# Window attention with sinks, then a highway layer: five placements changed in one hand-ordered instruction stream

## The chip, the cores and the metric

The kernel runs on one core of one Trainium2 chip. The metric is the device time of one execution in microseconds (us), given as a median over several runs. The core has a matrix engine (TensorE, in the profile PE for products and PEld for its weight loads), a vector engine (VectorE, DVE), an activation engine (ScalarE, ACT), a general engine (GpSimd, POOL) and a queue engine (SyncE, SP). Each of them takes its own instructions in order; DMA transfers are issued by POOL, SP and ACT.

## The reference

Four batches of eight heads, 768 positions, 64 values a head. A query at position i may look at the keys 0 to 3 (the sinks) and at the keys i-127 to i. What comes out is laid side by side for the eight heads, 3072 rows of 512, and goes through a highway layer.

```python
scores = scale * np.matmul(q, k.transpose(0, 1, 3, 2))
keep = is_sink | in_window
scores = np.where(keep, scores, -1000000000.0)
a = np.exp(scores - np.max(scores, axis=-1, keepdims=True))
a = a / (np.sum(a, axis=-1, keepdims=True) + 1e-09)
x = np.matmul(a, v)                       # then (tokens, 512)
H = np.maximum(x @ w_h, 0.0)
T = 1.0 / (1.0 + np.exp(-(x @ w_t + b_t)))
out = T * H + (1.0 - T) * x
```

## The kernel before, in words

The rows are cut into 24 tiles of 128 (n = 0 to 23, six for each batch b, c = n mod 6 within it). A tile goes through these steps, each a small function that the diff and the prediction name:

- `load_part`, `load_whole`, `load_v`, `load_v_third`: DMAs that POOL issues (L123, L130, L168, L161); they turn fp32 into fp16 on the way. `thirds[3]`, `thirds[4]` and `thirds[5]` are the three loads of v of batch 1.
- `transpose_qk` (L148) and `transpose_tiles` (L155): DVE turns q and k in 32x32 blocks.
- `scores` (L303, PE, into the one score buffer `ps_s`), `expo` (L334, ACT, from `ps_s` into `E`), `mask` (L342, DVE, `E` times a 0/1 mask, in place).
- `values` (L371 and L374, PE: the tile before and the tile itself times v, with a column of ones that gives the sum) and `values_of_sinks` (L357, PE: the sinks' part, for tiles with c of 2 or more), both into `ps_v`; `norm` (L383, L384, DVE) divides by the sum and gives `X`.
- `x_transpose` (L411, PE), `x_copy` (L416, ACT), `bias` and `gate` (L421, L425, PE, with the weights `wt`, into `ps_z`), `tanh` (L449, ACT), `hidden` (L465, PE, with `wh`, into `ps_h`), `diff` (L469, DVE; for some tiles L477 on ACT and L480 on DVE), the gate's value (`gate_on_act`, L455, on ACT or `gate_value`, L460, on POOL), `gated` (L483, DVE), `add` (L487, POOL), `store` (L491, SP).

For the sinks there are three helpers. `sink_keys(b)` (L264) lays out the keys of the sinks for `sink_scores` (L316), which scores four tiles of a batch at once at the loop step whose n2 is 3 past the batch's first tile. `sink_values(b)` (L280) multiplies the sinks' rows of v, which lie in `vs_rows`, by a mask and writes the 128x520 tile `vs[b]`; `values_of_sinks` reads it from the batch's third tile on. `keep_warm(n)` (L212) issues n products of zeros on PE.

The order of every engine is the order of the text: a last pass ties each instruction to the one before it on its engine. So the program is written out by hand for tiles 0 to 5 (the head), runs as a loop from s = 5 to 21 in which tile n2 = s+2 is scored, n1 = s+1 gets its values, n0 = s its gate and hidden products and n9 = s-1, n8 = s-2 are finished, and is written out again for the last two tiles. In the loop, POOL does in each step `add(n8)`, `gate_value(n9)`, and then what the tables `keys` and `loads` hold for n2.

In the head POOL issues a list of loads (`fill`) in two pieces. The second piece contains `sink_values(2)` ahead of the four loads of k's first half of batch 1 and `sink_values(3)` ahead of the fourth of these. The DMAs that POOL issues count on eight completion counters in turn, so each of them waits for the DMA that was issued eight before it.

Around the change, DVE's order in the head is `norm(1)`, `mask(2)`, `transpose_qk(0, 2, 1, 0, 8)` (the third segment of k of batch 0, which holds tiles 4 and 5), `mask(3)`, `norm(2)`, and PE's is `scores(3)`, `x_transpose(1)`, three idle products, `scores(4)`, `values(2)`, `gate(0)`. At the end, the last tile is gated in two halves of 256 columns; the first one's sum goes to POOL and SP, the second one's stays on DVE (L761, L763) and is stored by ACT's queue.

Of the kernel before, what the change touches and what calls it, by code (L numbers as in the profile page):

```python
# [30 lines left out]
def kernel(  # L31
# [14 lines left out]
    pe, act, dve, pool, sp = nc.tensor, nc.scalar, nc.vector, nc.gpsimd, nc.sync  # L46
# [9 lines left out]
    NC = S // P  # L56
    N = B * NC
    KC = DM // P
    G = 4
# [47 lines left out]
    def v_of(n):  # L107
        b, t = divmod(n, NC)
        return vt[b][t % TH3][:, :, t // TH3, :]
# [9 lines left out]
    def load_part(b, i, g, which, into=None, engine=pool):  # L119

        t0, nt = segments[b][which][i]
        into = nat[b][which][i] if into is None else into
        engine.dma_start(  # L123
            out=into[32 * g:32 * g + 32].rearrange("p hg m d -> p hg (m d)"),
            in_=(q, k)[which][b, :, t0:t0 + nt, :].rearrange(
                "(g hg) (r m) d -> g r hg (m d)", g=G, m=nt // 32)[g])
# [12 lines left out]
    def part_loads(b, i, which):  # L139

        return [lambda g=g: load_part(b, i, g, which) for g in range(G)]

    def transpose_qk(b, i, which, lo, hi):

        t0, nt = segments[b][which][i]
        dst = tr[b].bitcast(FP32).rearrange("p w hg t e -> p w hg (t e)")[
            :, which, :, t0:t0 + nt].rearrange("p hg (r m) -> p hg m r", m=nt // 32)
        dve.transpose(out=dst[:, :, lo:hi, :],  # L148
                      in_=nat[b][which][i].bitcast(FP32)[:, :, lo:hi, :])
# [15 lines left out]
    def load_v(n):  # L165

        b, t = divmod(n, NC)
        pool.dma_start(out=v_of(n)[:, :, 0:D],  # L168
                       in_=v[b, :, t * P:(t + 1) * P, :].transpose([1, 0, 2]))
# [40 lines left out]
    def keep_warm(n):  # L210
        for i in range(n):
            pe.matmul(ps_h, lhsT=zeros[:, 0:P], rhs=zeros[:, 0:DM], start=True, stop=True)  # L212
# [20 lines left out]
    for n, tile_v in enumerate([tile_v for of_batch in vt for tile_v in of_batch]):  # L233
        if n < 2:
            dve.memset(tile_v[:, :, :, D:D + 1], 1.0)
        else:
# [5 lines left out]
                       fill=0.0, base=0, pattern=[[1, P]], channel_multiplier=-1)  # L242
    pool.affine_select(out=mask_std[:, P:], in_=mask_std[:, P:], compare_op=ALU.is_ge,
                       fill=0.0, base=-1, pattern=[[-1, P]], channel_multiplier=1)
# [17 lines left out]
    def sink_keys(b, engine=pool):  # L262
        for hg in range(HG):
            engine.tensor_tensor(  # L264
                out=sk[:, b, hg, :, 0:H * NSINK].rearrange("p e (h s) -> p e h s", s=NSINK),
                in0=tr[b][:, 1, hg, 0:NSINK, :].rearrange("p s e -> p e s").unsqueeze(2)
                .to_broadcast([P, 2, H, NSINK]),
                in1=skmask[:, hg].unsqueeze(1).unsqueeze(3)
                .to_broadcast([P, 2, H, NSINK]), op=ALU.mult)
# [9 lines left out]
    def sink_values(b, engine=dve):  # L279
        engine.tensor_tensor(  # L280
            out=vs[b], in0=vs_rows[:, b].unsqueeze(1).to_broadcast([P, H, D + 1]),
            in1=vmask.unsqueeze(2).to_broadcast([P, H, D + 1]), op=ALU.mult)
# [54 lines left out]
    def mask(n):  # L337
        c = n % NC
        nq = 2 if c + 1 < NC else 1
        m = mask_0 if c == 0 else mask_std  # L340
        e3 = E[n].rearrange("p g hg x -> p (g hg) x")[:, :, 0:nq * P]
        return dve.tensor_tensor(  # L342
            out=e3, in0=e3, in1=m[:, 0:nq * P].unsqueeze(1).to_broadcast([P, H, nq * P]),
            op=ALU.mult)


    def av_of(n):
        if n < N - 1:
            return ps_v[:, :, 0:FREE]
        return ps_s[:, 2:4].rearrange("p b hg x -> p b (hg x)")[:, :, 0:FREE]  # L350
# [28 lines left out]
    def norm(n):  # L379
        rec = work.tile([P, 2, HB], FP32, tag="rec", name="rec")  # L380
        X[n] = work.tile([P, 2, HB, D], FP16, tag="X", name="X", bufs=10)
        av = av_of(n).rearrange("p i (j e) -> p i j e", e=D + 1)
        dve.reciprocal(out=rec, in_=av[:, :, :, D])  # L383
        dve.tensor_tensor(out=X[n], in0=av[:, :, :, 0:D],  # L384
                          in1=rec.unsqueeze(3).to_broadcast([P, 2, HB, D]), op=ALU.mult)
# [5 lines left out]
    HALVES = [slice(0, DM // 2), slice(DM // 2, DM)]  # L391

    def z_of(n, cols):
        return ps_z[:, cols] if n < N - 1 or cols == HALVES[1] else ps_v[:, 0, cols]
# [23 lines left out]
    def bias(n, cols=ALL, group=None):  # L418
        lhsT, rhs = (ones, brow) if group is None else (
            ones_g[32 * group:32 * group + 1], brow[32 * group:32 * group + 1])  # L420
        pe.matmul(z_of(n, cols), lhsT=lhsT, rhs=rhs[:, cols], start=True, stop=False)  # L421
# [12 lines left out]
    def outputs(n):  # L434
        TH[n] = work.tile([P, DM], FP16, tag="TH", name="TH", bufs=6)
        DD[n] = work.tile([P, DM], FP16, tag="DD", name="DD", bufs=8)
        if O[n] is None:
            O[n] = work.tile([P, DM], FP32, tag="O", name="O", bufs=10)
# [43 lines left out]
    def gated(n, cols=ALL):  # L482
        return dve.tensor_tensor(out=DD[n][:, cols], in0=DD[n][:, cols], in1=TH[n][:, cols],  # L483
                                 op=ALU.mult)

    def add(n, cols=ALL):
        return pool.tensor_tensor(out=O[n][:, cols], in0=DD[n][:, cols],  # L487
                                  in1=flat(X[n])[:, cols], op=ALU.add)

    def store(n, cols=ALL, after=None):  # L490
        behind(sp.dma_start(out=out[n * P:(n + 1) * P, cols], in_=O[n][:, cols]), after)  # L491

    def finish(n, cols=ALL):
        add(n, cols)
        store(n, cols)
# [21 lines left out]
    def v_thirds(b):  # L517
# [4 lines left out]
        ((6, 1), (7, 3), (8, 3), (9, 2), (10, 1), (11, 2), (12, 2), (13, 2), (14, 2), (15, 2),  # L522
         (16, 1), (17, 1)))

    keys = {8: 1, 12: 2, 18: 3}


    stored = {12: 1, 13: 3, 14: 4, 15: 6, 16: 7, 17: 9, 18: 10, 19: 12, 20: 14, 21: 16, 22: 18,
# [3 lines left out]
    thirds = [None] * TH3 + v_thirds(1)  # L532
    fill = part_loads(0, 1, 0) + part_loads(0, 1, 1)
# [2 lines left out]
        lambda: pool.dma_start(out=wt, in_=moe_w_t.rearrange("(kc p) of -> p kc of", p=P)),  # L536
        lambda: load_v(3), lambda: load_v(4),
        lambda: pool.dma_start(out=wh, in_=moe_w_h.rearrange("(kc p) of -> p kc of", p=P))]
    fill += part_loads(1, 0, 0)
    for work_item in fill:  # L540
        work_item()

    fill = [lambda: sink_values(2, engine=pool)] + part_loads(1, 0, 1)
    fill.insert(4, lambda: sink_values(3, engine=pool))
    fill += [lambda: load_v(5), thirds[3]] + part_loads(1, 1, 0) + [thirds[4]]

    act.copy(out=mask_0, in_=mask_std)
    act.copy(out=mask_0[0:NSINK, :], in_=ones_v.rearrange("p h i o -> p (h i o)")[
# [20 lines left out]
    repeat_sink_values()  # L569
    norm(0)  # L570
    copy_sink_values()
    for work_item in fill:
        work_item()
    sink_expo(0)
    x_transpose(0)
    x_copy(0)
# [6 lines left out]
    outputs(0)  # L583
    norm(1)
    act.copy(out=brow, in_=b32)
    mask(2)
    scores(3)
    expo(3)
    x_transpose(1)
    x_copy(1)  # L590
    transpose_qk(0, 2, 1, 0, 8)
    keep_warm(3)
    scores(4)
    mask(3)
    bias(0, group=3)
# [17 lines left out]
    gate(1)  # L613
    tanh(1, gate_too=False)
    mask(5)
    sink_values(1)
    x_transpose(3)
    x_copy(3)
    gate_on_act(0)
# [39 lines left out]
    thirds[5]()  # L659
    diff(2)  # L660
    gated(2)
    norm(5)
    add(2)
    hidden(3)
# [6 lines left out]
    for s in range(5, N - 2):  # L671


        n2, n1, n0, n9, n8 = s + 2, s + 1, s, s - 1, s - 2
        x_transpose(n0)
        x_copy(n0)

        hidden(n9, parts=range(2, KC))
        if n2 % NC == 3:
            sinks(n2 // NC)  # L680
        if not at_once(n9):
            gate_on_act(n9)
        take_hidden(n9)

        scores(n2)
        bias(n0, group=(n1 % NC + 1) % G)
        values_of_sinks(n1)
        expo(n2)

        if n1 not in ADDED:  # L690
            mask(n1)
        gated(n8)
        if n9 in TAKEN:
            diff_of_taken(n9)
        else:
            diff(n9)
        outputs(n0)
        values(n1)
        gate(n0, parts=range(0, 2))
        norm(n1)  # L700

        if n2 in keys and n2 < NC * 2:
            sink_keys(keys[n2])
        last = add(n8)
        while done < stored.get(n2, 0):
            store(done, after=last)
            done += 1
        gate_value(n9)
        if n2 in keys and n2 >= NC * 2:
            sink_keys(keys[n2])  # L710
        for load in loads[n2]:
            load()
        for piece in pieces[n2]:
            transpose_qk(*piece)
        for part in tiles[n2]:
            transpose_tiles(*part)
        if n2 == N - 1:
            mask(n2)
        gate(n0, parts=range(2, KC))
        tanh(n0, gate_too=at_once(n0))  # L720
        hidden(n0, parts=range(0, 2))

    n1, n0, n9, n8 = N - 1, N - 2, N - 3, N - 4
# [2 lines left out]
    x_copy(n0)  # L726
    hidden(n9, parts=range(2, KC))
    gate_on_act(n9)
    outputs(n1)
    bias(n0, group=(n1 % NC + 1) % G)  # L730
    values_of_sinks(n1)
    bias(n1, HALVES[0], group=(n1 % NC + 3) % G)
    values(n1)
    gated(n8)
    finish(n8)
# [11 lines left out]
    diff(n0)  # L747
    gated(n0)
    finish(n0)
    bias(n1, HALVES[1])  # L750
    for i, cols in enumerate(HALVES):
        gate(n1, cols)
        tanh(n1, cols, gate_too=(i == 0))
        hidden(n1, cols)
        diff(n1, cols)
        if i == 0:
            gated(n1, cols)
            finish(n1, cols)

    cols = HALVES[1]  # L760
    dve.scalar_tensor_tensor(out=DD[n1][:, cols], in0=TH[n1][:, cols], scalar=1.0,  # L761
# [39 lines left out]
```

## Time and profile before

| what | value |
|---|---|
| median of 3 runs | 109.62 us (108.58 to 110.47) |
| profiled execution, its own time | 109.37 us |
| its span | 107.6 us |
| mean clock granted to TensorE | 0.982 |
| busy: PE, DVE, ACT, POOL | 95.7, 93.8, 82.6, 86.0 us |
| `sink_values` on POOL | 2 instructions, 3.1 us |
| `sink_values` on DVE | 2 instructions, 1.4 us |
| `mask`, 128x2048 with the standard mask | 16 instructions, mean 1261 ns |
| idle products of 128x512 | 33, 9.5 us |

The span is what the profiler recorded between the first and the last instruction; the profiled execution took 1.77 us more than that. In a row of the timeline the first number is the start in us from the span's beginning and the second the duration; "x4" is the number of instructions merged into the row, and what stands in brackets is the time the engine sat idle before it and who released it. A busy PE need not be a fast one: its clock has a row of its own on the page.

### The profile page before, as it was taken

The numbers are of one execution on the slowest core, as the hardware profiler recorded it, in microseconds if no ns is written. First come the engines' busy times: TensorE is split into PE (matmuls) and PEld (weight loads), VectorE is DVE, ScalarE is ACT, GpSimd is POOL, SyncE is SP. The second block draws the span as 40 slices with busy tenths as digits, with TensorE's granted clock in tenths as the row PEclk, the third lists the DMA queues.
The fourth block names the chain that finished last, engine by engine and source line by source line (L and its number), as shares of the span: only waits on it lengthen the run. The fifth ranks groups of instructions, "written<-read, shape, count | busy, mean of one in ns | idle before, by whom it ended". The sixth has DMA issues, their size and how long they took to land.

```text
span 107.6 us, 3031 instructions
## 1 busy us (share of the span) xinstructions
PE 95.7 (89%) x1195; PEld 50.7 (47%) x1195; DVE 93.8 (87%) x183; ACT 82.6 (77%) x113; POOL 86.0 (80%) x117
## 2 busy tenths in 40 slices
PE   5996768499998998999999999999999999999900
PEld 2343443344543554556555455565544564554600
DVE  5898899974899779999998999999989999898670
ACT  0943799675765799999979997998799988965900
POOL 6989999637999999998899999998946543664640
PEclk9999999958999999999999999999999999999999
DMA  2999999998899999999999999999999555235441
GB/s 78 271 212 171 138 119 177 176 200 142 81 123 181 186 112 107 157 156 170 112 97 76 211 249 186 217 263 169 235 207 158 201 195 190 100 106 195 173 155 62
DMA packets 45077, 17.53 MB, mean 163 GB/s; under 512 B 38532, under 2 KB 41348, under 8 KB 45064
## 3 DMA queue, kind: packets, MB, share of 16 engines
q0 software_dynamic: 40656, 9.97, 98.0%
q1 hardware_dynamic: 3944, 6.73, 17.7%
q10 hardware_dynamic: 464, 0.66, 2.2%
q8 instruction: 9, 0.15, 0.6%
q14 instruction: 4, 0.03, 0.1%
HBM read 21.01 MB, written 6.29 MB: 254 GB/s over the span
## 4 chain that ended last, share of the span: by engine, by line
PE 55%; DVE 24%; DMA 9%; ACT 3%; issue 3%; POOL 2%; DVEq 0%; POOLq 0%
PE ps_z L425 13%; PE ps_h L465 13%; DVE E L342 7%; PE ps_s L303 7%; PE ps_v L374 6%; PE ps_v L371 6%; DMA v<-in_v_dram 4%; DMA nat<-in_q_dram 4%; DVE X L384 4%; PE ps_v L411 4%; DVE tr L148 3%; DVE DD L483 3%; DVE tr L155 2%; PE ps_z L421 2%; PE ps_v L357 2%
## 5 line engine op out<-in xcount | busy, mean ns | idle before, releaser
L334 ACT ACTIVATE E<-ps_s 128x2048 f16<-128x2048 f32 (+1 forms) x24 | 41.6, 1735 | 5.8 <-PE ps_s L303 5.7
L487 POOL TENSOR_TENSOR O<-DD,X 128x512 f32<-128x512 f16 (+1 forms) x19 | 22.3, 1176 | 13.1 <-DVE DD L483 12.6
L465 PE MATMUL ps_h<-wh,XT 128*128 128x512 f16 (+1 forms) x96 | 27.3, 375 | 0.0
L425 PE MATMUL ps_z<-wt,XT 128*128 128x512 f16 (+1 forms) x96 | 24.8, 382 | 0.0
L342 DVE TENSOR_TENSOR E<-E,mask_std 128x2048 f16<-128x2048 f16 (+1 forms) x20 | 23.1, 1156 | 0.5 <-ACT E L334 0.3
L449 ACT ACTIVATE TH<-ps_z 128x512 f16<-128x512 f32 (+1 forms) x24 | 14.1, 587 | 7.5 <-PE ps_z L425 7.4
L303 PE MATMUL ps_s<-tr 32*128 32x256 f16 (+1 forms) x384 | 14.5, 267 | 3.3 <-DVE tr L148 2.9
L384 DVE TENSOR_TENSOR X<-ps_v,rec 128x512 f16<-128x512 f32 x23 | 15.9, 692 | 0.8
L374 PE MATMUL ps_v<-v,E 128*128 128x65 f16 x184 | 13.7, 195 | 1.0 <-DVE E L342 0.5
L416 ACT COPY XT<-ps_v 128x512 f16<-128x512 f16 x23 | 13.4, 583 | 1.3 <-PE ps_v L411 0.8
L303 PEld LDWEIGHTS <-tr 32*128 32x128 f16 x384 | 7.9, 94 | 12.5 <-issue 6.4
L371 PE MATMUL ps_v<-v,E 128*128 128x65 f16 x152 | 13.3, 196 | 0.4 <-ACT XT L416 0.3
L374 PEld LDWEIGHTS <-E 128*128 128x128 f16 x192 | 11.8, 98 | 3.6 <-DVE E L342 2.5
L371 PEld LDWEIGHTS <-E 128*128 128x128 f16 x160 | 10.8, 98 | 5.1 <-issue 5.1
L148 DVE STREAM_TRANSPOSE tr<-nat 128x512 f32<-128x512 f32 (+1 forms) x14 | 12.7, 947 | 0.5 <-DMA nat<-in_q_dram 0.3
L465 PEld LDWEIGHTS <-XT 128*128 128x128 f16 x100 | 8.9, 98 | 6.1 <-issue 0.2
L123 POOL DMA_DIRECT2D nat<-in_k_dram x16 | 8.9, 566 | 3.5 <-DMA v<-in_v_dram 1.8
L469 DVE SCALAR_TENSOR_TENSOR DD<-ps_h,X 128x512 f16<-128x512 f32 (+1 forms) x16 | 10.6, 665 | 1.0 <-PE ps_h L465 0.8
L425 PEld LDWEIGHTS <-XT 128*128 128x128 f16 x100 | 8.4, 98 | 6.6 <-ACT XT L416 0.3
L161 POOL DMA_DIRECT2D v<-in_v_dram x9 | 10.7, 1190 | 0.0
L483 DVE TENSOR_TENSOR DD<-DD,TH 128x512 f16<-128x512 f16 (+1 forms) x24 | 10.4, 435 | 0.3
L212 PE MATMUL ps_h<-zeros 128*128 128x512 f16 x33 | 9.5, 442 | 1.3 <-DVE ones_v L217 1.3
(89 smaller groups left out, 141.8 us busy)
## 6 DMA issues: line engine op xcount, KB each, us to landing
out_dram<-O SPq DMA_DIRECT2D x18, 256.0 KB
v<-in_v_dram POOLq DMA_DIRECT2D x9, 256.0 KB, 6.4
nat<-in_q_dram POOLq DMA_DIRECT2D x8, 192.0 KB, 5.3
nat<-in_k_dram POOLq DMA_DIRECT2D x8, 192.0 KB, 5.4
out_dram<-first SPq DMA_DIRECT2D x4, 256.0 KB
v<-in_v_dram POOLq DMA_DIRECT2D x6, 128.0 KB, 5.0
nat<-in_q_dram POOLq DMA_DIRECT2D x8, 96.0 KB, 7.5
nat<-in_k_dram POOLq DMA_DIRECT2D x8, 96.0 KB, 4.2
```

The source lines that it names most:

```text
L148: dve.transpose(out=dst[:, :, lo:hi, :], in_=nat[b][which][i].bitcast(FP32)[:, :, lo:hi, :])
L303: pe.matmul(ps_s[:, g, hg, 0:nq * P], lhsT=tr[b][rows, 1, hg, c * P:(c + 1) * P, e], rhs=tr[b][rows, 0, hg, c * P:(c + nq) * P, e], start= ...
L334: act.activation(out=E[n][:, :, :, 0:nq * P], in_=ps_s[:, :, :, 0:nq * P], func=AF.Exp, scale=SCALE)
L342: return dve.tensor_tensor(out=e3, in0=e3, in1=m[:, 0:nq * P].unsqueeze(1).to_broadcast([P, H, nq * P]), op=ALU.mult)
L371: pe.matmul(slot, lhsT=E[n - 1][:, g, hg, P:2 * P], rhs=v_of(n - 1)[:, h, :], start=first, stop=False, skip_group_check=True)
L374: pe.matmul(slot, lhsT=E[n][:, g, hg, 0:P], rhs=v_of(n)[:, h, :], start=first, stop=True, skip_group_check=True)
L384: dve.tensor_tensor(out=X[n], in0=av[:, :, :, 0:D], in1=rec.unsqueeze(3).to_broadcast([P, 2, HB, D]), op=ALU.mult)
L425: pe.matmul(z_of(n, cols), lhsT=XT[n][:, kc * P:(kc + 1) * P], rhs=wt[:, kc, cols], start=False, stop=(kc == KC - 1))
L449: act.activation(out=TH[n][:, cols], in_=z_of(n, cols), func=AF.Tanh, scale=0.5)
L465: pe.matmul(h_of(n, cols), lhsT=XT[n][:, kc * P:(kc + 1) * P], rhs=wh[:, kc, cols], start=(kc == 0), stop=(kc == KC - 1))
L483: return dve.tensor_tensor(out=DD[n][:, cols], in0=DD[n][:, cols], in1=TH[n][:, cols], op=ALU.mult)
L487: return pool.tensor_tensor(out=O[n][:, cols], in0=DD[n][:, cols], in1=flat(X[n])[:, cols], op=ALU.add)
```

## The change

Six things move or are added, and what is computed stays the same:

1. `sink_values(2)` and `sink_values(3)` leave POOL's list of loads in the head. They are issued by POOL in the loop, at n2 = 12 and 18, ahead of that step's loads.
2. `sink_keys(2)` and `sink_keys(3)`, which stood at n2 = 12 and 18, go to n2 = 13 and 19.
3. `sink_values(1)` on DVE moves from behind `mask(5)` to behind `gated(2)`, ahead of `norm(5)`.
4. `transpose_qk(0, 2, 1, 0, 8)` on DVE goes ahead of `mask(2)`.
5. The idle products ahead of `scores(4)` are seven instead of three.
6. At the end, the first half's `bias` of the last tile goes from ahead of `values` to behind the last full `hidden`, and both halves use the plain bias rows; `gated` and `finish` of the first half come behind the second half's `diff`.

```diff
-    keys = {8: 1, 12: 2, 18: 3}
+    keys = {8: 1, 13: 2, 19: 3}
+    rows = {12: 2, 18: 3}
...
-    fill += part_loads(1, 0, 0)
+    fill += part_loads(1, 0, 0) + part_loads(1, 0, 1) + [lambda: load_v(5), thirds[3]]
+    fill += part_loads(1, 1, 0) + [thirds[4]]
...
-    fill = [lambda: sink_values(2, engine=pool)] + part_loads(1, 0, 1)
-    fill.insert(4, lambda: sink_values(3, engine=pool))
-    fill += [lambda: load_v(5), thirds[3]] + part_loads(1, 1, 0) + [thirds[4]]
...
     norm(1)
     act.copy(out=brow, in_=b32)
+    transpose_qk(0, 2, 1, 0, 8)
     mask(2)
     scores(3)
     expo(3)
     x_transpose(1)
     x_copy(1)
-    transpose_qk(0, 2, 1, 0, 8)
-    keep_warm(3)
+    keep_warm(7)
     scores(4)
...
     mask(5)
-    sink_values(1)
...
     gated(2)
+    sink_values(1)
     norm(5)
...
         if n2 in keys and n2 >= NC * 2:
             sink_keys(keys[n2])
+        if n2 in rows:
+            sink_values(rows[n2], engine=pool)
...
-    outputs(n1)
     bias(n0, group=(n1 % NC + 1) % G)
     values_of_sinks(n1)
-    bias(n1, HALVES[0], group=(n1 % NC + 3) % G)
     values(n1)
...
-    bias(n1, HALVES[1])
+    outputs(n1)
+    for cols in HALVES:
+        bias(n1, cols)
     for i, cols in enumerate(HALVES):
         gate(n1, cols)
         tanh(n1, cols, gate_too=(i == 0))
         hidden(n1, cols)
         diff(n1, cols)
-        if i == 0:
-            gated(n1, cols)
-            finish(n1, cols)
+    gated(n1, HALVES[0])
+    finish(n1, HALVES[0])
```

More of the change, by code (lines that the diff above doesn't have):

```diff
@@ L571 @@
     copy_sink_values()
-    for work_item in fill:
-        work_item()
     sink_expo(0)
```

## The prediction

> **What bounds the kernel now.** I read the shares of the chain that ended last first, then the granted clock in 40 slices (2.7 us each).
>
> ```profile
> PEclk9999999958999999999999999999999999999999
> ...
> PE 55%; DVE 24%; DMA 9%; ACT 3%; issue 3%; POOL 2%; DVEq 0%; POOLq 0%
> ```
>
> PE carries most of the chain, DVE a quarter, POOL 2%, so work on POOL costs nothing by itself; it can cost where it gets in the way of DVE or is late for somebody. The clock is full but for one dip, at 21.8 to 25.2 us by finer windows (0.50 granted). So I took the timeline of that stretch.
>
> ```profile
> 17.23 1.99 DVE L342 TENSOR_TENSOR E<-E,mask_std 128x2048 f16<-128x2048 f16 x1
> ...
> 18.06 2.07 POOL L280 TENSOR_TENSOR vs<-vs_rows,vmask 128x520 f16<-128x520 f16 x1
> 19.14 1.09 DVE L148 STREAM_TRANSPOSE tr<-nat 128x512 f32<-128x512 f32 x1
> ...
> 20.29 0.63 PE L303 MATMUL ps_s<-tr 32*128 32x256 f16 x16 [1.64 <-DVE tr L148]
> ...
> 21.10 0.59 POOL L123 DMA_DIRECT2D nat<-in_k_dram  x1 [0.97 <-DMA wt<-in_moe_w_t_dram]
> ...
> 24.61 1.07 POOL L280 TENSOR_TENSOR vs<-vs_rows,vmask 128x520 f16<-128x520 f16 x1
> ```
>
> Two things are to be seen. `mask(2)` took 1.99 us where masks of its size mostly take 1.18 to 1.29, and `sink_values(2)` took 2.07 where the next one took 1.07: they overlap, and both lost. And `scores(4)` waited 1.64 us for the transposition behind that mask; the clock halved 1.5 us after that wait.
>
> For the loop I followed the chain in order of time, and beside it POOL's timeline.
>
> ```profile
> 59.12 1.24 DVE E L342
> ...
> 62.49 1.23 DVE E L342
> 63.77 0.20 PE ps_v L374
> ```
>
> ```profile
> 38.78 2.28 POOL L487 TENSOR_TENSOR first<-DD,X 128x512 f32<-128x512 f16 x2
> ...
> 58.73 0.54 POOL L264 TENSOR_TENSOR sk<-tr,skmask 128x64 f16<-128x64 f16 x2
> ...
> 62.02 0.61 POOL L460 TENSOR_SCALAR TH<-TH 128x512 f16<-128x512 f16 x1
> 62.59 0.76 POOL L130 DMA_DIRECT2D nat<-in_q_dram  x1
> ```
>
> From 57.5 to 63.8, and again from 78.3 to 84.4, the chain is DVE's alone, so whatever lengthens a mask there moves the end. POOL has no idle time from 26.3 to 50 and hardly any from 53.8 to 71. The steps of the loop last 3.4 us.
>
> Last, DVE's timeline at the end.
>
> ```profile
> 102.11 0.94 DVE L483 TENSOR_TENSOR DD<-DD,TH 128x256 f16<-128x256 f16 x1
> 102.97 0.41 DVE L469 SCALAR_TENSOR_TENSOR DD<-ps_h,X 128x256 f16<-128x256 f32 x1
> 103.49 0.59 DVE L761 SCALAR_TENSOR_TENSOR DD<-TH,DD 128x256 f16<-128x256 f16 x1
> ```
>
> A product of 256 columns took 0.94 where 512 columns take 0.41: a POOL sum ran from 101.75 to 102.90, and the product ended 0.15 after it. So a DVE product of two SBUF tiles that starts while POOL computes ends about its own length after POOL.
>
> **The parts.**
>
> *Head, POOL's list.* Taking both products out frees 2.07 + 1.07 us of POOL, but not earlier loads: the load behind the first waits for `wt` (21.10), the one behind the second for an older load too (26.33, after 0.65 of idle). Those waits fill the room, so every later load leaves when it did. Value 0; bounds 0 and -0.65 (the last wait, were it to shrink).
>
> *Head, transposition ahead of `mask(2)`.* Its data (issued up to 11.8, 3.5 to 4.3 to land) is there at 15.4. It would run 17.23 to 18.2, `mask(2)` 18.2 to 19.4 (1.2 without POOL beside it). Then `scores(4)` waits for the score buffer instead, which `expo(3)` (17.73 + 1.88) frees at 19.61: start 19.66, not 20.29, **-0.63**. The seven idle products run from 17.84 at 0.216 each to 19.35, under that same wait: 0. At half clock they would end at 20.85 and cost 1.2; the clock was 1.00 there. PE's idle stretch falls from 1.64 to 0.3, so I take the dip to be gone: `gate(0)` 0.63 shorter, the values, copies and x-transposes behind it some 0.2 each. `gate(0)` needs `wt`, landed about 21.0; `norm(3)`, now at 25.77, would come 1.5 earlier. What is late next is `wh`: issued 15.17, 10.9 to land, so `hidden(0)`, now at 26.99, can't start before 26.1. Head gain at that point: **-0.9**.
>
> The Trainium skill (TensorE: Matmul & The Clock Gate, Part 1) says that the clock halves after an idle window of about 3.4 us. Here it halved after 1.64 us of waiting, though for 3.4 us, so the trace differs on what it takes; taken literally, the idle products would matter in neither kernel.
>
> *What POOL gives back.* POOL's stretch from 26.3 to 50 doesn't move. The mask at 41.52 would start at 40.6, while the second of the sums at 38.78 runs until 41.06, and wait 0.43. Kept of the head: **-0.45** (0 to -0.9). The loads of batch 1 hold: the last of k lands at 39.3 and is turned at 39.7.
>
> *`sink_values(1)` on DVE.* 0.69 leaves a place where DVE waits for PE anyway and goes to 35.0, in front of a 0.57 wait of `norm(5)`: 0, bounds -0.1 and +0.15.
>
> *Loop, `sink_values(2)`.* It takes the place of the 0.54 at 58.73, lasts 1.07, ends at 59.80. The mask at 59.04 on the chain waits for it: 0.76 instead of the 0.14 that it lost to the two short ones (1.32 against 1.18). **+0.6**; by the head's row (1.99 against 1.22) 0.77 - 0.14, the same. Queued behind it on POOL are two loads of q and the next sum.
>
> The Trainium skill (SBUF — State Buffer, Who interferes with whom) calls this an exclusive lock on a shared port: the first instruction holds it, the other blocks wholly. The row at 102.11 agrees; the one at 17.23 doesn't, where the mask was first and still lost 0.77. By that rule the cost here is the same 0.6, since the sinks' product is first.
>
> *Loop, `sink_keys(2)` one step on.* Its 0.54 falls behind the 0.61 that ends at 62.63, just as the next mask (62.41, then about 63.0) waits: 0 if the mask goes first, +0.53 if it doesn't. I take **+0.25**. Sinks' scores need it three and more us later: no wait. The last load of q for batch 3 (62.59 + 5.7 = 68.3, used at 69.03) leaves 1.1 later, with its use 0.8 later: 0.4 of slack. That of k (69.20 + 6.1 = 75.3, used at 75.80) keeps 0.2.
>
> *Loop, batch 3.* `sink_values(3)` at 78.81 ends at 79.88, the mask starts at 79.83: **+0.05**, bound 0.77. `sink_keys(3)` follows at 83.27, with a mask from 83.06: **+0.25** (0 to 0.53).
>
> *End.* The first half's bias leaves a place ahead of the last `values` (0.22 on the chain) and costs 0.11 later, which hides partly under ACT's copy: **-0.1**. The second half's `diff` no longer stands behind the blocked 0.94: it starts at 102.3, the first half's product at 102.6 waits out POOL until 102.75 and ends near 103.0; then L761 and L763 (0.3 + 0.42) contend with POOL's last sum (0.67) and end between 103.7 and 104.3, against 104.53. The first half's store, before at 103.8 with 0.7 to spare, comes at 103.8 to 104.4 and may now be the last one. **-0.25**, bounds -0.75 and +0.3.
>
> **Sum:** -0.45 + 0.6 + 0.25 + 0.05 + 0.25 - 0.1 - 0.25 = +0.35 on the profiled execution's own 109.37: **109.7 us**. That execution lies 0.25 below the median of the runs shown, 109.62, so the change would be hardly visible; about 2% (2.2 us) is what a measurement of this kernel can tell from no change.
>
> **The rivals.**
>
> *The products on POOL miss the masks.* The phases of POOL and DVE shift with the head's gain; if the sinks' work falls beside `norm` or a transposition (two at 58.41 and 58.73 overlap without loss), the loop costs 0.1, the head keeps 0.9, the end 0.6: 109.37 - 1.4 = 108.0. For it: no POOL operation lengthened the mask at 79.83. Against it: from 53.85 POOL's phase is set by DVE's own product, so 58.73 against 59.04 stays.
>
> *POOL becomes the bound* (the slower one). From 53.85 to 71 POOL has no room, so 1.07 more there makes it late for three or four steps; its gate value (0.61) then runs into the mask, about 0.3 a step, and the last load of k comes after its use. It decides once POOL lags DVE by 0.5, the slack of that load. 1.07 + 3 x 0.3 + 0.3 for batch 3 - 0.8 for head and end = +1.5: 110.9. For it: the rows without idle. Against it: DVE loses 0.6 by the same product, which takes up most of the lag.
>
> *The clock dip stays* with the shorter wait, so that part of the head does not do what it could: head gain 0, 110.15. For it: PE is some 70% busy from 21.7 on even then, with the waits for `wh` and the copies. Against it: stretches as busy (8 to 15 us, 5.1 of 7) kept full clock.
>
> **How the numbers follow.** Forecast 0.40, missed masks 0.25, POOL as the bound 0.25, dip 0.10. The unknown terms span -1.75 to +2.2 about the profiled time; with a median that moves by half a us from set to set, 108.0 to 111.3 leaves out the outer tenth on either side. Faster by over 2% (under 107.4) needs the first rival and luck: 0.06. Slower by over 2% (over 111.8) is the tail of the second: 0.10. Within: 0.84.
>
> **What would show it.** `scores(4)` starting at 19.7 with the buffer, not the transposition, as releaser; no slice with a clock under 9 after the start; the load behind the first removed product still at 21.1 behind `wt`; `hidden(0)` near 26.1; the mask beside POOL's L280 in the loop 1.8 to 2.0 long; L763 ending near 104.2 less whatever was won before it. I am wrong if the loop's masks stay at 1.2, if DVE's transpositions start to wait for DMA near 69 to 76, or if the clock drops elsewhere.

## The result, and the profile after

The changed kernel takes 112.31 us (median of 6 runs, 112.11 to 113.54); the kernel before took 109.3 beside it. The ratio is 1.032, with a 95% interval of 1.025 to 1.039: slower, where the forecast was 109.7 and a range up to 111.3. The profiled execution took 112.46 us, its span is 110.7. Medians here are of all executions; ratios leave out those more than 1.5% above the fastest of their kernel.

On the page of the changed kernel, the row of the granted clock, the shares of the chain that ended last, and one group of instructions (operation, then busy us, mean ns and idle time before it):

```profile
PEclk9999999999999999999999999999999999999999
...
PE 42%; POOL 18%; DVE 17%; ACT 11%; DMA 5%; issue 3%; ACTq 1%; DVEq 0%
...
L460 POOL TENSOR_SCALAR TH<-TH 128x512 f16<-128x512 f16 x12 | 10.8, 900 | 0.0
```

The dip of the clock is gone from this execution, as forecast; its mean granted clock is 0.998 against 0.982, so the clock is not what made it slower. But POOL, which had 2% of the chain, has 18%, and the gate value's mean is 900 ns where each took about 610 before. The chain in order of time shows where (start, duration, what):

```profile
60.21 1.27 POOL O L487
61.48 0.59 POOL TH L460
62.07 1.66 POOL sk L264 x2
63.73 1.42 POOL nat L130 x2
65.16 1.17 POOL O L487
66.33 1.57 POOL TH L460
67.89 1.44 POOL nat L130 x2
...
79.09 1.05 POOL TH L460
```

From 60.2 to 80.1 us the chain runs along POOL without a gap. To see what that cost I laid the starts of the masks of the two traces beside each other. They mark the loop's steps, and mask n is that of tile n:

| mask of tile | before, start | after, start | after minus before |
|---|---|---|---|
| 11 | 55.63 | 54.56 | -1.07 |
| 12 | 59.04 | 57.97 | -1.07 |
| 13 | 62.41 | 61.85 | -0.56 |
| 14 | 65.91 | 65.40 | -0.51 |
| 15 | 69.65 | 70.34 | +0.69 |
| 16 | 73.03 | 74.26 | +1.23 |
| 17 | 76.42 | 78.90 | +2.48 |
| 18 | 79.83 | 82.57 | +2.74 |
| 19 | 83.06 | 86.64 | +3.58 |
| 20 | 86.55 | 90.18 | +3.63 |
| end of DVE's last instruction | 104.53 | 107.56 | +3.03 |

In this execution the head won 1.07, the loop lost 4.70 between masks 11 and 20, and the end won 0.56. That is, to 0.04, the whole of the 3.1 us between the spans. How the loop loses is in the rows of DVE's and POOL's timelines of the changed kernel (start, duration, instruction; in brackets idle time and releaser). First POOL:

```profile
57.65 1.05 POOL L280 TENSOR_TENSOR vs<-vs_rows,vmask 128x520 f16<-128x520 f16 x1
...
62.05 1.68 POOL L264 TENSOR_TENSOR sk<-tr,skmask 128x64 f16<-128x64 f16 x2
...
65.16 1.17 POOL L487 TENSOR_TENSOR O<-DD,X 128x512 f32<-128x512 f16 x1
66.29 1.60 POOL L460 TENSOR_SCALAR TH<-TH 128x512 f16<-128x512 f16 x1
...
86.84 1.68 POOL L264 TENSOR_TENSOR sk<-tr,skmask 128x64 f16<-128x64 f16 x2
...
89.78 0.62 POOL L460 TENSOR_SCALAR TH<-TH 128x512 f16<-128x512 f16 x1
```

Then DVE:

```profile
57.97 1.83 DVE L342 TENSOR_TENSOR E<-E,mask 128x2048 f16<-128x2048 f16 x1
...
61.85 1.30 DVE L342 TENSOR_TENSOR E<-E,mask_std 128x2048 f16<-128x2048 f16 x1
...
65.40 2.02 DVE L342 TENSOR_TENSOR E<-E,mask_std 128x2048 f16<-128x2048 f16 x1
67.93 0.42 DVE L483 TENSOR_TENSOR DD<-DD,TH 128x512 f16<-128x512 f16 x1 [0.51 <-POOL TH L460]
```

In the kernel before, the mask of the third of these rows, that of tile 14, stood so:

```profile
65.91 1.18 DVE L342 TENSOR_TENSOR E<-E,mask_std 128x2048 f16<-128x2048 f16 x1
```

The rows of the changed kernel are to be read in order of time. At 57.65 the sinks' product is first: the mask that starts at 57.97 ends 1.10 after it (59.80 against 58.70). At 61.85 the mask is first: the keys, 0.54 long in the loop of the kernel before, end 0.58 after it. From here POOL is late by 1.1 us, and that is enough for its next sum (65.16) to be running when the next mask starts. The mask ends 1.09 after the sum (67.42 against 66.33); the gate value, which follows the sum, gets its turn only after the mask and ends 0.47 after it (67.89); and `gated` on DVE, which before never waited for a gate value, waits 0.51 for this one. The later steps repeat it with gate values of 1.61, 1.61 and 1.07, each of which `gated` waits for; the mask itself is held up for long only in every second step (2.02, 1.27, 1.99 and, half as large, 0.75). While the loads last, POOL's own work of a step (1.17 for the sum, 0.61 for the gate value, 1.2 to 1.9 for loads) leaves it at most 0.4 of the 3.4 us to catch up with, so one lag keeps making the next. I call this the lock. It ends at 81 us with the last load.

Of the 4.70, 0.51 went at the first meeting (mask 12 to 13), 3.30 in the lock (mask 13 to 18) and 0.84 at the mask beside `sink_values(3)` (mask 18 to 19). The trace also shows what slack does. At 86.84 the keys of the last batch start 0.20 behind a mask and take 1.68 once more; but no loads are left, POOL had idled 1.51 us just before that step's sum, the next gate value takes 0.62, and the step loses 0.05.

The Trainium skill (SBUF — State Buffer, Who interferes with whom) states that a VectorE instruction with two SBUF inputs contends with a GpSimd instruction that reads SBUF, that the port they share is an exclusive lock, and that the order of issue decides who waits. The loop's rows agree with it in both orders: a mask ends 1.09 or 1.10 after the POOL instruction where it takes 1.18 alone, the keys end 0.58 after the mask where they take 0.54, the gate value 0.47 where it takes 0.61.

### The profile page after: what moved, and what is told of

Same layout as the page of the kernel before. It is cut to its first block, busy times and chain, and to the rows that moved or that the text cites. A ratio compares the mean times of both kernels' runs of the same rounds, so it can differ in the third digit from the quotient of the medians.

```text
span 110.7 us, 3039 instructions
## 1 busy us (share of the span) xinstructions
PE 96.2 (87%) x1199; PEld 50.4 (46%) x1199; DVE 96.3 (87%) x183; ACT 83.2 (75%) x113; POOL 90.3 (82%) x117
## 4 chain that ended last, share of the span: by engine, by line
PE 42%; POOL 18%; DVE 17%; ACT 11%; DMA 5%; issue 3%; ACTq 1%; DVEq 0%
PE ps_h L465 10%; PE ps_z L425 9%; ACT E L334 9%; PE ps_s L303 7%; POOL TH L460 6%; POOL O L487 5%; DMA first<-in_q_dram 5%; DVE E L342 4%; PE ps_v L371 4%; PE ps_v L374 4%; DVE tr L148 3%; POOL nat L130 3%; PE ps_v L411 3%; DVE X L384 3%; POOL v L161 2%
## 5 line engine op out<-in xcount | busy, mean ns | idle before, releaser
L342 DVE TENSOR_TENSOR E<-E,mask_std 128x2048 f16<-128x2048 f16 (+1 forms) x20 | 24.4, 1219 | 1.0 <-ACT E L334 0.8
L425 PE MATMUL ps_z<-wt,XT 128*128 128x512 f16 (+1 forms) x96 | 24.2, 374 | 0.0
L212 PE MATMUL ps_h<-zeros 128*128 128x512 f16 x37 | 10.3, 431 | 1.3 <-DVE ones_v L217 1.3
L460 POOL TENSOR_SCALAR TH<-TH 128x512 f16<-128x512 f16 x12 | 10.8, 900 | 0.0
```

Of the source, the lines that this page charges most:

```text
L342: return dve.tensor_tensor(out=e3, in0=e3, in1=m[:, 0:nq * P].unsqueeze(1).to_broadcast([P, H, nq * P]), op=ALU.mult)
L425: pe.matmul(z_of(n, cols), lhsT=XT[n][:, kc * P:(kc + 1) * P], rhs=wt[:, kc, cols], start=False, stop=(kc == KC - 1))
L460: pool.tensor_scalar(out=TH[n], in0=TH[n], scalar1=0.5, scalar2=0.5, op0=ALU.mult, op1=ALU.add)
```

## The experiments

Theory A is the lock just described. Theory B is that POOL was only short of throughput, and theory C that the new order of the head caused the loss. Since the head turned out to vary from one profiled execution to the next, each kernel's trace is also read by the time from mask 11 to mask 20: 30.92 us before, 35.62 in the changed kernel.

**The sinks' part alone**, on the kernel before:

```diff
-    keys = {8: 1, 12: 2, 18: 3}
+    keys = {8: 1, 13: 2, 19: 3}
+    rows = {12: 2, 18: 3}
...
-    fill = [lambda: sink_values(2, engine=pool)] + part_loads(1, 0, 1)
-    fill.insert(4, lambda: sink_values(3, engine=pool))
+    fill = part_loads(1, 0, 1)
...
+        if n2 in rows:
+            sink_values(rows[n2], engine=pool)
```

> The kernel before with the sinks' part of the change alone: both products of the sinks' values leave the list of loads in the head and go into the loop at n2 = 12 and 18, the sinks' keys one step later. Theory A (POOL and the masks lock into each other): from the shifts between the two traces the loop loses 4.7 us between 58 and 91 us, and the head wins at most 0.8 because its mask no longer has a POOL product beside it: 109.3 + 4.7 - 0.8 = 113.2, with gate values of 1.6 us on POOL in four steps. Theory B (POOL is only short of throughput): 1.07 us more in the first busy stretch and nothing in the second, where POOL idles: 110.0. Theory C (the loss comes from the head's new order, which shifts the phases): this kernel stays within 1 us of 109.3.

Measured: 113.78 us, ratio 1.042 (1.033 to 1.050); from mask 11 to mask 20 35.63 us, the changed kernel's 35.62 to a hundredth. C falls, and so does B: 4.7 us is more than twice the work that was added to the loop (two products of 1.06).

**The sinks' part undone**, in the changed kernel (the same lines turned back):

> The changed kernel with the sinks' part undone: products of the sinks' values in the head's list and the keys at n2 = 12 and 18 as before; the transposition ahead of the mask, the idle products, the later product for batch 1 and the plainer end stay. Theory A: the head's and the end's gains stay, 1.1 and 0.55 us by the two traces, less what the head's POOL product takes back from the mask: 107.6 to 108.3. Theory C: near 112.

Measured: 109.34 us beside 109.33, ratio 0.998 (0.993 to 1.003); mask 11 to mask 20 is 30.93. The lock is gone, so the whole slowdown belongs to the sinks' part. But theory A had put this kernel at 107.6 to 108.3, and that failed: the gains of the head are gone too. At mask 11 this trace stands 0.47 behind the kernel before, where the changed kernel's stood 1.07 ahead. Here is nearly all of that, in its timeline:

```profile
30.69 1.22 POOL L487 TENSOR_TENSOR first<-DD,X 128x512 f32<-128x512 f16 x1
31.15 1.05 DVE L483 TENSOR_TENSOR DD<-DD,TH 128x512 f16<-128x512 f16 x1
34.04 1.18 POOL L487 TENSOR_TENSOR first<-DD,X 128x512 f32<-128x512 f16 x1
34.25 1.26 DVE L483 TENSOR_TENSOR DD<-DD,TH 128x512 f16<-128x512 f16 x1
```

Two products of 0.41 meet POOL sums and lose 0.64 and 0.85. POOL's first sum stands behind its list of loads and starts at 30.69 here, at 32.25 in the kernel before and at 31.88 in the changed one, so whom it meets on DVE differs from trace to trace.

**The keys alone**, one step later, the products of the sinks' values staying in the head: no work is added anywhere.

```diff
-    keys = {8: 1, 12: 2, 18: 3}
+    keys = {8: 1, 13: 2, 19: 3}
```

> The kernel before with only the sinks' keys moved, from n2 = 12 and 18 to 13 and 19; no work is added to the loop. Theory A in the form that the blocked keys start it (in the changed kernel's trace they took 1.68 us for 0.54, because a mask had started 0.2 us ahead): POOL falls 1.1 us behind and the lock follows, 111 to 112.5. Theory A in the form that it needs the added product as well: under 109.9. Theory B: 109.3.

Measured: 112.9 us, ratio 1.033 (1.025 to 1.041), as slow as the whole change. B falls for good. The two engines' rows in its trace, in order of time:

```profile
62.29 1.29 DVE L342 TENSOR_TENSOR E<-E,mask_std 128x2048 f16<-128x2048 f16 x1
62.48 1.68 POOL L264 TENSOR_TENSOR sk<-tr,skmask 128x64 f16<-128x64 f16 x2
...
65.59 1.17 POOL L487 TENSOR_TENSOR O<-DD,X 128x512 f32<-128x512 f16 x1
65.83 2.02 DVE L342 TENSOR_TENSOR E<-E,mask_std 128x2048 f16<-128x2048 f16 x1
66.73 1.60 POOL L460 TENSOR_SCALAR TH<-TH 128x512 f16<-128x512 f16 x1
```

The keys start 0.19 us behind a mask and end 0.58 behind its end; the sum and the gate value follow just as in the changed kernel. Mask 11 to mask 20 takes 34.13 us, 3.2 more than before; between masks 13 and 18 the loss is 3.29, the 3.30 of the changed kernel.

**The values alone**, in the loop behind the keys, which stay where they were:

```diff
+    rows = {12: 2, 18: 3}
...
-    fill = [lambda: sink_values(2, engine=pool)] + part_loads(1, 0, 1)
-    fill.insert(4, lambda: sink_values(3, engine=pool))
+    fill = part_loads(1, 0, 1)
...
             sink_keys(keys[n2])
+        if n2 in rows:
+            sink_values(rows[n2], engine=pool)
```

> The kernel before with the products of the sinks' values moved into the loop at n2 = 12 and 18, behind the sinks' keys, which stay in those steps. POOL gets the same work in the loop as in the changed kernel, but no keys between a gate value and the loads. Theory A with the blocked keys as its start: POOL falls 1.1 us behind in one step and one mask waits, but the keys aren't blocked: 109.3 + 0.5 (mask) + about 0.5 - 0.8 (head) = 109.5, at most 111. Theory A with any lag of a microsecond as its start: 112 to 113.5, as with the keys moved. Theory B: 110.0.

Measured: 114.33, 114.64 and 114.91 us in three executions and 110.62 in the fourth, too far apart for a ratio. In the profiled one, of 114.64, the product started 0.20 behind a mask and took 2.13, and the lock ran from there (mask 11 to mask 20: 36.78). So it does not take the keys in their later step. The time of the fourth suggests that this kernel locks in some executions and not in others; it has no trace, so that is not shown.

**A write that nobody reads**, put on POOL once, where the moved keys had stood, in the kernel before; first long, then short:

```diff
+    lag = const.tile([P, 1152], FP16, tag="lag")
...
         gate_value(n9)
+        if n2 == 13:
+            pool.memset(lag, 0.0)
```

> The kernel before, untouched but for one POOL write of 1152 columns to a tile that nobody reads, some 1.05 us by the memsets of the head (128 columns 0.20, 256 columns 0.31), once, at n2 = 13 behind the gate value: where the moved keys stood. It reads nothing and nobody waits for it. Theory A (one lag of about a microsecond on POOL is enough: the next sum runs into the mask, the mask into the gate value, and so on): near the kernel with the keys moved, 112 to 113. Theory B (throughput): 109.3, at most 109.9. Theory D (it takes a POOL product that competes with the mask): 109.3 to 109.9.

> The same with 512 columns, about 0.5 us. Theory A: POOL had an idle of some 0.1 us a step at most before 71 us, so a lag of 0.5 us lives on, but the sum of the next step ends 0.5 us later, at 65.9, just as that step's mask starts: no lock, 109.3 to 110. If it locks as well, the kernel before stands right at the edge. Theories B and D: 109.3.

Measured: 112.04 us for the long one, ratio 1.027 (1.018 to 1.035); 110.48 for the short one, ratio 1.011 (1.002 to 1.020). POOL's timeline of the long one (its lines are numbered one higher, for the line added):

```profile
62.45 1.05 POOL L711 MEMSET lag<- 128x1152 f16 x1
...
64.94 1.17 POOL L488 TENSOR_TENSOR O<-DD,X 128x512 f32<-128x512 f16 x1
66.07 1.61 POOL L461 TENSOR_SCALAR TH<-TH 128x512 f16<-128x512 f16 x1
```

The write itself runs at its expected 1.05 beside a mask of 1.29 (62.27), where the keys, which read, took 1.68. Yet 1.05 us of lateness, once, with nothing waiting for it, starts the same lock (33.77 from mask 11 to mask 20). With half of it one mask waits (that of tile 14, 1.47), but no gate value is longer than 0.63 and the loop loses 0.33. The total of 110.48 lies above the 109.3 to 110 foreseen; in the profiled execution the rest of the excess, 0.87, was there at mask 11, before the write. So a lag alone is enough: it takes neither the keys' work nor a first meeting at the port. Theory D falls, and the point from which the lock runs lies, for this place in the loop, between 0.5 and 1.05 us of lag.

**The keys on DVE**, in the later steps, so that POOL keeps its pace:

```diff
-    keys = {8: 1, 12: 2, 18: 3}
+    keys = {8: 1, 13: 2, 19: 3}
...
-            sink_keys(keys[n2])
+            sink_keys(keys[n2], engine=dve)
```

> The sinks' keys of the last two batches at n2 = 13 and 19, as in the kernel that moved only the keys, but done by DVE (two of about 0.2 us in each step) instead of POOL. Theory A: POOL keeps its pace, no lock; DVE is on the chain there and pays 0.4 us in each of the two steps: 109.3 to 110.1. A theory by which the later keys themselves are what is waited for (by the sinks' scores two steps on): 112 to 113, as with POOL.

Measured: 110.71 us, ratio 1.012 (1.007 to 1.018). No lock: all gate values are 0.61 or 0.62. DVE pays 1.32 between mask 11 and mask 20, not 0.8, which puts the total above the 109.3 to 110.1 foreseen. The keys' later step as such is not what costs the 3.3%.

**One POOL operation fewer** in the changed kernel, the gate value of tile 11:

```diff
-        return n < 7 or n in (9, 15) or n >= N - 3
+        return n < 7 or n in (9, 11, 15) or n >= N - 3
```

> The changed kernel with one POOL operation fewer: the gate value of tile 11 (0.61 us on POOL, in the step in which the changed kernel's trace shows the first gate value of 1.60) is made by ACT. Theory A (lock): with no gate value there for the mask to hold up, POOL gets back 1.6 us at once, its next sum starts clear of the mask, and of the 3.8 us lost in the first stretch some 2.3 come back: 110.0. Theory B (throughput): POOL has 0.6 us less to do: 111.7.

Measured: 110.3 us, ratio 1.008 (1.004 to 1.012) to before. The two engines in that step and the next:

```profile
66.63 1.17 POOL L487 TENSOR_TENSOR O<-DD,X 128x512 f32<-128x512 f16 x1
66.87 2.02 DVE L342 TENSOR_TENSOR E<-E,mask_std 128x2048 f16<-128x2048 f16 x1
68.82 0.41 DVE L483 TENSOR_TENSOR DD<-DD,TH 128x512 f16<-128x512 f16 x1
69.31 1.16 POOL L487 TENSOR_TENSOR O<-DD,X 128x512 f32<-128x512 f16 x1
70.44 0.62 POOL L460 TENSOR_SCALAR TH<-TH 128x512 f16<-128x512 f16 x1
71.21 1.18 DVE L342 TENSOR_TENSOR E<-E,mask_std 128x2048 f16<-128x2048 f16 x1
```

The first sum still holds up a mask, but no gate value queues behind it; a step later sum and gate value end 0.15 before the mask starts, and that is all it takes. The loop's loss falls from 4.70 to 1.23: taking 0.61 us off POOL won back 3.5. Of this 2.65 is the lock (mask 13 to 18 loses 0.65, not 3.30); most of the rest is `sink_values(3)`, which now misses the mask.

**The new end alone**, on the kernel before (the last hunks of the diff):

> The kernel before with the new end alone (the first half's bias later and plain, its product and sum behind the second half's difference). From the two traces, the distance from the last full mask of the loop to the end fell by 0.56 us: 108.7, a ratio of 0.995. If the first half's store, which now leaves later, is the last to land: 109.2.

Measured: 109.14 us beside 109.42, ratio 0.992 (0.987 to 0.998). The medians are 0.3% apart and the ratio says 0.8%, so the total alone hardly shows a gain. The stage is firmer evidence: from the start of the last mask to DVE's last instruction it takes 7.77 us, as in every kernel here with the new end, against 8.33 or 8.34 in every one with the old. To the end of the span it is 11.0 against 11.4.

**The head's order alone**: the transposition ahead of the mask and seven idle products, on the kernel before.

```diff
+    transpose_qk(0, 2, 1, 0, 8)
     mask(2)
...
-    transpose_qk(0, 2, 1, 0, 8)
-    keep_warm(3)
+    keep_warm(7)
```

> The kernel before with the transposition ahead of the mask and seven idle products, and nothing else. At the mask of tile 5, at 25 us, it is 1.0 us ahead of before. If that stays, 108.3. If the sums on POOL, whose start the landing of the loads sets, run into DVE's products between 31 and 36 us, as in the kernel with the sinks' part undone (two products of 1.05 and 1.26 us for 0.41), all of it is lost: 109.2 to 109.5.

Measured: 109.91 us beside 109.42, ratio 1.002 (0.997 to 1.007): nothing. In its trace the sums meet no product of DVE; instead three transpositions wait for their loads (0.47, 0.81 and 0.69 us between 31 and 42). In these traces what is won before 30 us is lost to what comes next, here the loads, there the sums.

**The sinks' products on DVE in the head**, with the keys at their old steps and all other parts of the change:

```diff
     mask(4)
+    sink_values(2)
...
     mask(5)
+    sink_values(3)
```

> The changed kernel with the keys back at n2 = 12 and 18 and the products of the sinks' values of the last two batches on DVE in the head, behind the masks of tiles 4 and 5, where DVE waited 0.81 and 0.76 us in the changed kernel's trace (each product 0.69). No POOL product in the head to meet a mask, none added in the loop. Theory A: the head's 1.1 us and the end's 0.55 us both stay: 107.7. If what the head wins is always taken back by POOL before 50 us, as when the sinks' part was undone: 108.8.

Measured: 109.45 us beside 109.12, ratio 0.996 (0.991 to 1.001). No lock, and no measurable gain: the 107.7 of theory A did not come. In the profiled execution (109.91) the last load of k of batch 3 landed after 7.5 us, not 6.1, and the transposition at 77.03 on DVE waited 0.86 for it.

**The first two sums later**, on top of that, with `sink_values(1)` ahead of `gated(2)`:

```diff
-    add(0)
     for load in part_loads(1, 1, 1):
...
-    add(1)
     loads[6][0]()
     thirds[5]()
+    add(0)
+    add(1)
     diff(2)
-    gated(2)
     sink_values(1)
+    gated(2)
```

> The kernel with the sinks' products on DVE in the head, and the first two sums on POOL put behind the loads that follow them, so that they don't run beside DVE's products of tiles 1 and 2 (0.98 and 1.26 us there for 0.41). If these meetings are what ate the head's microsecond, it stays now, with the end's half: 107.7 to 108.2. If the sums only meet other products of DVE: 109.0 to 109.5.

Measured: 110.73, 110.96, 112.97 and 113.27 us, each above the median of the kernel before (109.42). The sums now stand three in a row, and one product of DVE met all of them:

```profile
36.79 4.12 DVE L483 TENSOR_TENSOR DD<-DD,TH 128x512 f16<-128x512 f16 x1
37.25 3.37 POOL L487 TENSOR_TENSOR first<-DD,X 128x512 f32<-128x512 f16 x3
```

It took 4.12 us for 0.41. At mask 11 this trace is 2.09 behind the kernel before, and from mask 11 to mask 20 it takes the same 30.92, so what this kernel loses, it loses in the head. The repair made the meeting worse.

## Why the prediction was wrong, step by step

- *Head, POOL's list: 0.* Right: in the changed kernel the first load behind the removed product starts at 21.10 behind `wt`, to the hundredth where it started before; the one behind the second at 26.02 instead of 26.33, within the bound.
- *Head, order and idle products: -0.9, of which -0.45 kept.* The steps happened: `scores(4)` at 19.86 behind `expo(3)`, no dip, `hidden(0)` at 25.78 (forecast 26.1). POOL gave back less than the 0.45 forecast: the mask at 40.30 took 1.25 for 1.21, and 1.07 was kept, beyond the bound of 0.9. But it is a gain of this execution, not of the change. The same head stood, against the kernel before, at -1.07 at mask 11 in the changed kernel and at +0.39 in the kernel with the gate value on ACT; and with the old head unchanged the values run from -0.14 to +0.87. The new order of the head with the old loop gave ratios of 0.998 (with the new end) and 1.002 (without). I had taken the landings and POOL's phase of one execution as fixed.
- *`sink_values(1)` on DVE: 0.* Right: from `gated(2)` to `norm(5)` it is 0.99 us in both traces.
- *`sink_values(2)` in the loop: +0.6.* Right: mask 1.83 where 1.8 to 2.0 was forecast, and 0.51 lost by the next mask. That holds in the changed kernel; behind keys left in its step (the values alone) the same product was blocked itself, took 2.13, and a lock followed.
- *`sink_keys(2)` one step on: +0.25.* **This step failed.** I asked what the keys do to the mask and answered 0 if the mask goes first. The mask did go first, and then it is POOL that pays: 1.1 us of lag, which the sum had no term for. That lag started the lock, 3.30 us where this term said 0.25; the loop as a whole lost 4.70 where the sum had 1.15. Alone, this edit costs 3.3%. The order could have been read off the kernel before: there the gate value ends 0.22 after that mask starts (62.63 against 62.41), and in the changed kernel again (62.07 against 61.85), since both move together. The prediction moved the mask to 63.0 and left the gate value at 62.63.
- *Batch 3: +0.05 and +0.25.* The 0.05 rested on a distance of 0.05 us between two rows; after the lock the phases were others, the product came first by 0.13, and the mask took 2.02: 0.84 lost, beyond the bound of 0.77. The keys behind it cost 0.05, not 0.25. That the two together stay under 0.77 and 0.53 is luck.
- *End: -0.35.* Right in kind, measured -0.56.
- *The slower rival, POOL as the bound: 110.9, at 0.25.* It came nearest to the mechanism: I named the place and the gate value that runs into the mask. Its lag of 0.5 us was the slack of a load of k, and no load was waited for; that the runs put the point of the lock between 0.5 and 1.05 is luck. Nor had I the price: 1.07 + 3 x 0.3 + 0.3 = 2.3 for the loop against 4.7 measured. The 0.3 a step was the mask's wait alone. A meeting has two sides: the mask loses up to 0.84 to the sum (2.02 against 1.18), the gate value loses 1.0 to the mask, and `gated` then waits 0.51. And I had held against it that DVE's loss takes up POOL's lag; in fact both engines lose in the same step, so POOL stays late: its sum starts 0.24 to 0.99 ahead of the mask in these steps, against 1.78 to 2.15 in the kernel before.

The loads, for which the prediction feared, weren't the cause: none of DVE's transpositions in the changed kernel's loop waits for one.

## What to carry to other kernels

Where two engines exclude each other at a port, price a moved instruction from both sides: who starts first, and what the one that loses holds up next. If the loser's engine has no slack in a step, a single lag of a third of a step can last for as long as the slack is missing, and neither its work nor its wait shows the price; look for the slack first and keep such an instruction out of steps that have none. A gain read from one execution's phases is not a gain until runs with other phases show it.

## What the runs showed that I had not expected

- One write of 1.05 us that nothing waits for costs 2.7% (1.8 to 3.5), since it lengthens the loop by 2.85 us; half of it leaves the loop all but untouched (0.33).
- A DVE product can wait for a whole queue of POOL sums: 4.12 us beside three in a row, though it had started 0.46 us ahead of the first in the records, and it ended 0.29 after the last of them. In the loop a mask does get in between a sum and the gate value behind it. What makes the difference stays open.
- In the head the loser isn't always one side: `mask(2)` beside a sinks' product on POOL took 1.99 us in the kernel before, with 2.07 for the product, and 2.61 where the keys were on DVE (1.15 for the product), while with the new end alone it took 1.21 with 1.36 for the product. In the second the mask ends 1.10 after the product, as if it had come last, though it starts 0.36 ahead of it in the records. An exclusion in order of recorded start doesn't give the first two; no run settles it.
- The mean granted clock differs between executions of one kernel, and the time goes with it. Of the 61 executions of the kernel before that were measured beside the experiments, the 14 with a mean of 0.981 or less have a median of 110.9 us, the 17 with 0.995 or more one of 108.9. Seven idle products in place of three don't end this: the executions with the new order of the head alone lie between 0.980 and 1.000 too, those with the sinks' part undone between 0.982 and 0.999. Whether a dip makes an execution longer, or a late load makes both the dip and the length, isn't settled by any run here.
